# A causal attention with a soft mixture of experts on one core: a new hand-written order of its operations, ordered turns between POOL and VectorE, a third query buffer, the combine softmax in the expert stage, and output in full rows

## The chip, the core and the metric

The kernel runs on one core of a Trainium2 chip. A core has a matrix engine (TensorE; PE in the profile, its weight loads PEld), three elementwise engines (VectorE or DVE, ScalarE or ACT, GpSimd or POOL), and SyncE (SP), which here only issues transfers to the 16 DMA engines. Each engine works through its own instructions in order; between engines there are semaphores. SBUF is the memory of 128 partitions that the engines work on, PSUM is what TensorE writes, in banks of 2 KB a partition. The metric is device time in microseconds of one execution.

## The reference

```python
# q, k, v: (8, 8, 576, 64) = B, H, S, D;  all float32
scores = 1/sqrt(D) * q @ k.T          # causal mask, softmax over keys
local = softmax(scores) @ v
q_p = where(q > 0, q, exp(q) - 1) + 1
mem_out = (q_p @ M_prev) / (q_p . z_prev + 1e-6)
g = sigmoid(beta)                      # one a head
attn = g * mem_out + (1 - g) * local   # -> x: (4608, 512), heads beside each other
# soft mixture of experts: 8 experts, 4 slots each
logits = x @ phi                       # (4608, 32)
d = softmax(logits, axis=0); slot_input = d.T @ x
slot_out[e] = relu(slot_input[e] @ w1[e]) @ w2[e]      # w1 (512, 1024), w2 (1024, 512)
c = softmax(logits, axis=1)            # the combine softmax
out = c @ slot_out                     # (4608, 512)
```

## The kernel before

**Attention.** The 64 heads are worked through as 32 pairs (`n` = 0 to 31: 8 batches of 4 pairs; a pair fills 128 partitions with two heads of 64). For each pair three loads come in on SyncE: q, k (`qk`) and v (`vv`, with M_prev beside it). POOL splits q and k each into a rounded part and a remainder (`op_qhi`, `op_kn` by line 363, `op_qlo` line 394, `op_kl` line 400; into the one tile `X` and the one tile `K2`), so that the scores are three matmuls (line 409, in two groups sA and sB, each in the two banks-of-two `psS0` and `psS1`). VectorE adds the mask and takes the extreme of each row (`op_max`, line 444), out of PSUM; ScalarE takes the exponentials with their sums (`op_exp`, line 453). TensorE transposes the result (`op_t`, line 545), and ScalarE or VectorE copies it out of PSUM (`op_te`, lines 358 and 361) into the one tile `at`, from which the products with v are made (`op_av`, line 572).

**The two normalizers and FR.** Neither part is divided before its product. From the sums (`op_rec`) and the memory norm, factors of a row each are made, turned to lie along a row (`op_rt`, `op_rf`), written to DRAM (`op_rrw`, three transfers, lines 472 and 473), and read back to all partitions (`op_rrr`, line 477: two transfers of 288 KB, tile `FR`, one buffer). FR has two uses: it scales the finished product (`op_mo` line 602, `op_xe` line 607), and its other half multiplies the features (`op_qn`, line 526, one instruction a head, on VectorE or POOL), into the part `C` of `at`, which takes the memory product into the same matmul `av.A`.

**The features.** `op_qmin` (line 482 on ScalarE, 484 on VectorE) writes min(q, 0) into one of two `qp` buffers (`n % 2`), `op_qexp` (line 487, ScalarE) takes its exp, `op_qphi` (line 491, VectorE) adds max(q, 0). Both inputs of `op_qphi` and of `op_qn` lie in SBUF. From the features `op_norm` (line 497, TensorE) makes the memory norm; `op_neps` scales it out of PSUM, `op_nmk` (line 508, POOL or VectorE) masks it, `op_nred` (lines 512 and 513) reduces it, `op_nrw` and `op_nrg` (517, 521, 522) take it through DRAM into `nG`, which `op_rf` uses.

**The slots.** Whenever a quarter of rows (512 of the 4608; `c0` to `c7`) is finished, `op_x1` makes its logits, `op_x1l` to `op_x1d` a running softmax over rows, `op_x3` and `op_x4` add to the slot inputs. `op_x2m`, `op_x2e`, `op_x2s` (lines 656 to 673: two VectorE instructions, one exp, four VectorE instructions), `op_x5` (a transpose, line 702) and `op_x5e` (a copy) make the combine softmax of that quarter, ready and turned, in `cT`. This is done so for seven quarters; the logits of the last two stay in `lt2`. `op_y1` to `op_y12` do the last half quarter and close the sums.

**The order.** All of this is one list, `SEQ` (lines 34 to 285): an entry names an operation, its pair or quarter behind the @, and the PSUM bank behind the colon. The program is emitted in the order of the list, and `pin()` (line 849) fixes it: on each engine every instruction is kept behind the one emitted ahead of it. `EV` says which engine (a, v, p for ScalarE, VectorE, POOL) does an operation that more than one can do. SyncE's transfers, weights (`w.`) too, stand in the same list. A pair takes about 78 entries.

**The experts.** 64 weight tiles of 512 KB (rows of 4 KB) are needed. 28 go to buffers of their own during attention, 17 to the attention's buffers as these come free, 19 to the first of the 28 once the first layer has used them. The first layer (`f1`, line 893), transposes (`f1t`, line 901) and the second layer (`f2`, line 910) follow each other on TensorE; the second layer is done for each half of the 512 output columns in turn (`dh` = 0, 1). In between stand `c1` (lines 914 to 927) and `c2`, which do the combine softmax of the quarters 7 and 8 with one transpose each way. `g1`, `g2` spread a finished half to `so`, and `comb(dh, t4)` (line 943) makes 512 rows of it: eight matmuls (line 949), one copy on ScalarE and one on VectorE, and one transfer of 512 KB in rows of 256 numbers, 1 KB (line 951).

## Time and profile before

| | |
|---|---|
| runs before | 533.03, 526.08, 535.86 us; median 533.03 us |
| the profiled execution | 531.52 us, of which the span from the first to the last instruction 529.4 us |
| mean granted TensorE clock | 0.964 |
| busy: PE, PEld, DVE, ACT, POOL | 452.6, 281.7, 405.2, 342.6, 195.1 us |
| moved | 86.2 MB read from HBM, 9.88 MB written |
| costliest groups | ScalarE exp (L453) 166.6 us, VectorE max (L444) 136.4, products with v (L572) 119.5, transposes (L545) 116.8, scores (L409) 93.1 |
| POOL | L400 47.4 us, L526 46.3, L394 45.4, L363 21.5 and 25.0 |

How to read the rows. A group has its line, engine, operation, the tiles out<-in, shapes, xcount, then busy time and the mean of one in ns, then the idle time of the engine just before it and what ended that. A row of waits has the waiting engine, tile and line, what it waited for, then us in total, times, and the longest. A row of windows has start:end, length, and for each engine busy us and (xinstructions), then the granted clock, the mean busy share of the DMA engines, and GB/s. A row of the timeline has its start, its duration, engine, line, operation, tiles, and in brackets the idle time before it with what ended it. A row by tile has durations ns as min/median/max, then the first and last start in us. "The chain" is the work that ended last, followed back from the end.

### The profile page before, as it was taken

The page shows a single profiled execution, that of the slowest core. Times are in us where ns is not written, and L with a number is a line of the kernel's source. Part 1 is how long each engine was busy: PE and PEld are TensorE (multiplying, and loading weights), DVE is VectorE, ACT ScalarE, POOL GpSimd, SP SyncE. Part 2 cuts the span into 40 slices and gives each one's busy share as a digit, 9 for nine tenths or more (in the row PEclk, how much of TensorE's full clock was granted, in tenths as well). Part 3 has the DMA queues.
Part 4 walks back from the last instruction along what each step waited for, and adds up shares of the span by engine and source line. Part 5 has one row for each costly group of instructions (what it writes and reads, how often), then busy time and mean ns, then how long its engine had stood idle before and what let it go on. Part 6 is the DMA issues. An engine that isn't in the chain of part 4 may idle for free.

```text
span 529.4 us, 13465 instructions
## 1 busy us (share of the span) xinstructions
PE 452.6 (85%) x4874; PEld 281.7 (53%) x4874; DVE 405.2 (77%) x1253; ACT 342.6 (65%) x983; POOL 195.1 (37%) x191
## 2 busy tenths in 40 slices
...
GB/s 218 109 114 163 126 151 251 97 113 180 106 83 164 145 233 169 92 247 112 162 153 250 89 189 117 187 114 145 141 164 167 125 156 241 357 361 407 337 293 303
DMA packets 44192, 96.96 MB, mean 183 GB/s; under 512 B 9184, under 2 KB 19424, under 8 KB 44128
## 3 DMA queue, kind: packets, MB, share of 16 engines
...
q10 hardware_dynamic: 288, 0.09, 0.1%
HBM read 86.22 MB, written 9.88 MB: 182 GB/s over the span
## 4 chain that ended last, share of the span: by engine, by line
PE 34%; DVE 21%; DMA 17%; ACT 9%; issue 7%; POOL 7%; SPq 3%; DVEq 0%; POOLq 0%; ACTq 0%
DMA FR<-rd 11%; PE psS L409 8%; PE psT L545 7%; DVE qp L491 6%; DVE sm L444 5%; PE oa L572 5%; POOL at L526 4%; PE pf L910 3%; ACT qp L482 2%; DVE at L361 2%; PE psT L497 2%; ACT qp L487 2%; PE pf L893 2%; PE pp L949 2%; ACT at L358 2%
## 5 line engine op out<-in xcount | busy, mean ns | idle before, releaser
L453 ACT ACTIVATE sm<-sm,nm 128x192 f32<-128x192 f32 (+4 forms) x288 | 166.6, 581 | 12.3 <-DVE nm L444 11.2
L444 DVE CUSTOM_DVE_ANT_0 sm<-psS,rm 128x320 f32<-128x320 f32 (+4 forms) x288 | 136.4, 509 | 13.2 <-PE psS L409 10.1
L572 PE MATMUL oa<-at,vv 128*32 128x512 f32 (+3 forms) x1280 | 119.5, 474 | 4.4 <-DVE at L526 2.3
L545 PE MATMUL psT<-cs,sm 128*128 128x128 f32 x768 | 116.8, 290 | 7.1 <-ACT at L358 2.4
L358 ACT COPY at<-psT 64x256 f32<-64x256 f32 (+3 forms) x223 | 91.0, 418 | 34.3 <-PE psT L545 16.7
L545 PEld LDWEIGHTS psT<-cs,sm 128*128 128x128 f32 x768 | 87.6, 147 | 40.4 <-issue 13.3
L526 POOL TENSOR_TENSOR at<-qp,FR 64x576 f32<-64x576 f32 x32 | 46.3, 1446 | 153.5 <-DMA FR<-rd 122.7
L409 PE MATMUL psS<-K,X 64*128 64x256 f32 (+2 forms) x960 | 93.1, 330 | 9.5 <-DVE nm L444 7.4
L409 PEld LDWEIGHTS psS<-K,X 64*128 64x128 f32 x960 | 75.2, 193 | 27.8 <-issue 17.2
L361 DVE COPY at<-psT 64x256 f32<-64x256 f32 (+3 forms) x169 | 74.5, 455 | 11.6 <-PE psT L545 5.5
L572 PEld LDWEIGHTS oa<-at,vv 128*32 128x32 f32 x1280 | 35.3, 110 | 42.8 <-issue 25.8
L453 ACT ACTIVATION_READ_ACCUMULATOR sm<-sm,nm 128x1 f32 x288 | 54.8, 190 | 0.0
L491 DVE SCALAR_TENSOR_TENSOR qp<-qk,qp 128x576 f32<-128x576 f32 x32 | 42.2, 1320 | 10.2 <-ACT qp L487 4.6
L400 POOL TENSOR_TENSOR K<-qk,K 128x576 fp32r<-128x576 f32 x32 | 47.4, 1482 | 1.2
L394 POOL TENSOR_TENSOR X<-qk,X 128x512 fp32r<-128x512 f32 x32 | 45.4, 1418 | 0.8
L482 ACT ACTIVATE qp<-qk 128x576 f32<-128x576 f32 x27 | 18.5, 684 | 39.8 <-POOL at L526 24.1
L363 POOL TENSOR_SCALAR X<-qk 128x512 fp32r<-128x512 f32 x32 | 21.5, 673 | 60.4 <-PE psS L409 34.4
L526 DVE TENSOR_TENSOR at<-qp,FR 64x576 f32<-64x576 f32 x32 | 37.9, 1183 | 3.2 <-DMA FR<-rd 2.9
L497 PE MATMUL psT<-qp,qk 128*32 128x144 f32 x256 | 15.2, 310 | 24.9 <-DVE qp L491 18.8
L363 POOL TENSOR_SCALAR K<-qk 128x576 fp32r<-128x576 f32 x32 | 25.0, 782 | 8.7 <-DMA qk<-in_k_dram 4.6
L502 ACT ACTIVATE rn<-psT,rm 128x144 f32<-128x144 f32 x19 | 9.0, 471 | 29.7 <-PE psT L497 28.2
L487 ACT ACTIVATE qp<-qp 128x576 f32<-128x576 f32 x32 | 21.9, 684 | 9.3 <-DVE qp L484 8.5
...
## 6 DMA issues: line engine op xcount, KB each, us to landing
...
```

Of the source, the lines that this page charges most:

```text
L358: nc.scalar.copy(o, i)
L361: nc.vector.tensor_copy(out=o, in_=i)
L363: ENG = dict(a=act, v=dve, p=lambda o, i: nc.gpsimd.tensor_scalar(out=o, in0=i, scalar1=1.0, scalar2=1.0, op0=ALU.mult, op1=ALU.mult))
L394: nc.gpsimd.tensor_tensor(out=X[:, 1, :], in0=st[n]["q"][:, 64:576], in1=X[:, 0, :].bitcast(F32), op=ALU.subtract)
L400: nc.gpsimd.tensor_tensor(out=K2[:, 1, :], in0=kt[:, 0:S], in1=K2[:, 0, :].bitcast(F32), op=ALU.subtract)
L409: nc.tensor.matmul(ps[h][:, a:e], X[ROW[h], x, 128 * i - 128:128 * i], K2[ROW[h], y, k0:k0 + e - a], start=(x, y) == (0, 0), stop=(x, y) = ...
L444: nc.vector.tensor_tensor_reduce(out=smt(n, i, h), in0=src, in1=msk, op0=ALU.add, op1=ALU.min, scale=-0.125, scalar=3.0e38, accum_out=s["n ...
L453: nc.scalar.activation(sm, sm, AF.Exp, scale=-1.0, bias=s["nm"][:, J:J + 1], accum_out=s["sum"][:, J:J + 1])
L491: nc.vector.scalar_tensor_tensor(out=t, in0=st[n]["q"], scalar=0.0, in1=t, op0=ALU.max, op1=ALU.add)
L526: ALU_ENG[ev(f"qn.{h}", n)].tensor_tensor(out=C[r, h, :], in0=st[n]["qp"][r], in1=FR[r, 1, :], op=ALU.mult)
L545: nc.tensor.transpose(out=ps[:, 128 * x:128 * x + 128], in_=win(n, i, h, c), identity=ident)
L572: nc.tensor.matmul(o[r, c0:c1], vt[:, n % 2, c, r], rhs[h], start=start, stop=stop)
```

## The change

1. **The list** `SEQ` and the engine choice `EV` are new throughout. Two and a half thousand entries stay, but for those of point 4. One stretch, from the scores of pair 12 to those of pair 13, before:

```
sA@12 te.A3y@10 te.A3@10 exp.2h0@11 mo@9 exp.a@11 sa@12 te.A1@10 te.AAy@10 rrr@10 t.A2@10:2 exp.2h1@11 x3.1@c2:0
max.1h0@12 te.A2@10 max.4h1@12 t.B3@10:1 exp.1h1@11 nrg@11 x5@c1:2 max.4h0@12 av.1@10 exp.4h1@11 loadk@13 max.a@12
max.1h1@12 te.B3y@10 x1d@c1 x3e.1@c2 sB@12 rec@11 exp.1h0@12 te.B3x@10 te.B3@10 exp.4h1@12 t.A1@11:0 x5e@c1 max.2h0@12
rt@11:1 exp.4h0@12 av.2@10 max.3h1@12 qn.0@10 rf@11 av.3@10 te.A1@11 max.2h1@12 rrw@11 t.A2@11:2 qn.1@10 x3.0@c2:1
kn@13 max.3h0@12 qmin@12 w.r12@0 ava@10:0 av.4@10 te.A2@11 kl@13 av.A@10 qexp@12 xe@10 qphi@12 t.B1@11:2 x3e.0@c2
mo@10 qhi@13 norm@12:0 te.B1@11 t.B3@11:1 qlo@13 neps@12 rrr@11 nmk@12 t.B2@11:0 exp.a@12 nred@12 t.A3@11:2 te.B3y@11
exp.2h0@12 te.B3@11
```

and after:

```
sA@12 x4a.1@c1 exp.2h1@11 te.A2@10 te.A3x@10 exp.3h0@11 te.A3y@10 sa@12 max.4h1@12 exp.3h1@11 t.AA@10:1 loadk@13
norm@12:2 max.a@12 av.2@10 te.AAx@10 rec@11 neps@12 max.1h1@12 te.AAy@10 exp.a@12 nmk@12 rt@11:0 max.1h0@12 t.B1@11:2
rf@11 exp.1h0@12 max.4h0@12 t.A1@11:1 rrw@11 te.B1@11 x3.1@c2:0 nred@12 exp.1h1@12 sB@12 qn.0@10 te.A1@11 nrw@12
qn.1@10 w.r9@0 av.3@10 kn@13 max.3h1@12 loadq@14 qmin@13 ava@10:2 av.A@10 max.3h0@12 qhi@13 x3e.1@c2 xe@10 t.B3@11:1
qexp@13 kl@13 mo@10 t.AA@11:0 te.B3@11 t.A3@11:2 te.B3y@11 exp.3h1@12 rrr@11 te.B3x@11 av.1@11 te.AAy@11 qlo@13
exp.3h0@12 te.A3@11 te.AAx@11 max.2h1@12 t.A2@11:1 te.A3y@11 nrg@12 exp.4h0@12 max.2h0@12 t.B2@11:0 te.A2@11
```

2. **Turns.** For qhi, qlo, kn, kl, qphi, qn and nmk, wherever two that follow each other in the list are on different ones of POOL and VectorE, the later waits for the earlier by a semaphore (`turn`). The list after has 123 such changes of engine. All qmin go to ScalarE (27 of 32 before), qphi can be on either engine and stays on VectorE in all 32; of the 64 qn 34 are on POOL (32 before); of the copies `te` 180 are on VectorE (165 before).

3. **Third query buffer**: `qp` has three buffers, `n % 3`.

4. **Combine softmax behind the experts.** `op_x2m`, `op_x2e`, `op_x2s`, `op_x5`, `op_x5e` and the second transpose of `op_x2` are gone. The logits stay in `cT`, and `c1`/`c2` do all nine quarters in the expert stage in batches of 4, 4 and 1.

5. **Output in full rows.** The weight buffers are allocated as pairs (`wv`). For the rows of `t4` < 2 (`EARLY`) both halves go out as before; for the seven others the two halves of the columns are put into one tile, and one transfer of 1 MB in rows of 2 KB goes out after the second half.

6. **Smaller.** The factors are laid out in 24 rows, so that `op_rrw` is two transfers in place of three; the DRAM tiles `nd` are three fixed ones whose ones are written at the start by three small transfers on ScalarE's queue.

```diff
-    qps = big.tile([128, 2, S], F32, name="qp")
+    qps = big.tile([128, 3, S], F32, name="qp")
...
+    nds = [drm.tile([2, 1088], F32, name=f"nd{i}", bufs=1) for i in range(3)]
...
+        for nd in nds:
+            nc.scalar.dma_start(out=nd[:, S:1088].rearrange("h (r x) -> h r x", x=128), in_=nG[0][0:8])
         nc.vector.memset(den, 0.0)
+        for t in sums:
+            nc.vector.memset(t, 1.0)
...
     def op_rrw(n):
         rf = st[n]["rf"]
-        rd = st[n]["rd"] = drm.tile([2, 2, S], F32, name="rd")
-        for t in range(2):
-            nc.sync.dma_start(out=rd[:, t, 64:S].rearrange("h (i x) -> h i x", i=4), in_=rf[9 * t:9 * t + 8])
-        nc.sync.dma_start(out=rd[:, :, 0:64].rearrange("h t x -> t h x"), in_=rf[8:18:9].rearrange("t (h x) -> t h x", h=2))
+        rd = st[n]["rd"] = drm.tile([2, 2 * S], F32, name="rd")
+        nc.sync.dma_start(out=rd[:, 64:1088].rearrange("h (r x) -> h r x", x=128), in_=rf[0:16])
+        nc.sync.dma_start(out=rd.rearrange("h (t x) -> t h x", x=64)[0:18:17], in_=rf[16:21:4].rearrange("t (h x) -> t h x", h=2))
...
     def op_qmin(n):
-        st[n]["qp"] = qps[:, n % 2]
+        st[n]["qp"] = qps[:, n % 3]
...
     def op_x2(qd):
...
-        if qd < 7:
-            nc.tensor.transpose(out=ps[:, 128:256], in_=d["lt"], identity=ident)
...
+    def wv(x):
+        if x // 2 == len(wdb):
+            wdb.append(wres.tile([128, 2048], F32, name=f"w{x // 2}"))
+        return wdb[x // 2][:, 1024 * (x % 2):1024 * (x % 2) + 1024]
...
+    port = [None]
+
+    def turn(i0, e):
+        for i in list(nc.cur_bb.bb.instructions)[i0:]:
+            if i.engine not in (mybir.EngineType.DVE, mybir.EngineType.Pool):
+                continue
+            if port[0] and port[0][0] != e:
+                tc.add_manual_dep(i, port[0][1], mybir.DependencyInfo(mybir.DependencyClass.Sync, mybir.DependencyReason.DATA), reason="port")
+            port[0] = (e, i.name)
+
...
         a = [int(x) if x.isdigit() and f not in ("w", "max", "exp") else x for x in a]
+        i0, pe = len(nc.cur_bb.bb.instructions), f in ("qhi", "qlo", "kn", "kl", "qphi", "qn", "nmk") and n != "y"
         if n == "y":
             ops[f](*(a or [0]))
         else:
             ops[f](int(n.lstrip("c")), *a)
+        if pe:
+            turn(i0, "p" if f[0] == "k" or f in ("qhi", "qlo") else ev(name.split("@")[0], int(n)))
     si = y["si"]
...
-    stage = [len(order) - nw + x % (NRES - len(order) + nw) for x in range(2 * NQ)]
+    nl = len(order) - nw
+    homes = [wdb[i // 2] for i in range(nl + nl % 2, NRES - 1, 2)] + [pieces[x][:, 0:2048] for x in PARTS if x in pieces]
+    single = [pieces[x] for x in ("X", "K2", "vv", "xk")]
...
-    def c1(qd):
+    cq_ = [(0, 4, at[:, 2048:2560]), (4, 8, acc), (8, 9, at[:, 2048:2560])]
+
+    def c1(x):
+        a, b, t = cq_[x]
+        w = 128 * (b - a)
+        c = cc[x] = t[:, 0:w]
         ps = psP.tile([128, 2, 512], F32, name="pp")[:, 0]
-        nc.tensor.transpose(out=ps[:, 0:128], in_=lt2[:, qd - 7, :], identity=ident)
-        lk = ps[:, 0:128].rearrange("a (j s) -> a j s", s=32)
-        m4 = sml.tile([128, 4], F32, name="m4")
-        nc.vector.reduce_max(out=m4, in_=lk, axis=AX.X)
-        c = cc[qd] = sml.tile([128, 4, 32], F32, name=f"c{qd}", bufs=1)
-        nc.vector.tensor_tensor(out=c, in0=lk, in1=m4.rearrange("a (j x) -> a j x", x=1).broadcast_to([128, 4, 32]), op=ALU.subtract)
+        for i in range(a, b):
+            nc.tensor.transpose(out=ps[:, 128 * (i - a):128 * (i - a) + 128], in_=cT[:, i, :], identity=ident)
+        g = lambda z: z.rearrange("a (j s) -> a j s", s=32)
+        one_ = lambda z: z.rearrange("a (j x) -> a j x", x=1).broadcast_to([128, 4 * (b - a), 32])
+        m4 = sml.tile([128, 16], F32, name="m4")[:, 0:4 * (b - a)]
+        nc.vector.reduce_max(out=m4, in_=g(ps[:, 0:w]), axis=AX.X)
+        nc.vector.tensor_tensor(out=g(c), in0=g(ps[:, 0:w]), in1=one_(m4), op=ALU.subtract)
         nc.scalar.activation(c, c, AF.Exp)
-        s4 = sml.tile([128, 4], F32, name="s4")
-        nc.vector.reduce_sum(out=s4, in_=c, axis=AX.X)
+        s4 = sml.tile([128, 16], F32, name="s4")[:, 0:4 * (b - a)]
+        nc.vector.reduce_sum(out=s4, in_=g(c), axis=AX.X)
         nc.vector.tensor_scalar(out=s4, in0=s4, scalar1=1e-9, scalar2=None, op0=ALU.add)
         nc.vector.reciprocal(out=s4, in_=s4)
-        nc.vector.tensor_tensor(out=c, in0=c, in1=s4.rearrange("a (j x) -> a j x", x=1).broadcast_to([128, 4, 32]), op=ALU.mult)
-
-    def c2(qd):
+        nc.vector.tensor_tensor(out=g(c), in0=g(c), in1=one_(s4), op=ALU.mult)
+
+    def c2(x):
+        a, b, t = cq_[x]
         ps = psP.tile([128, 2, 512], F32, name="pp")[:, 0]
-        nc.tensor.transpose(out=ps[:, 0:128], in_=cc[qd].rearrange("a j s -> a (j s)"), identity=ident)
-        act(cT[:, qd, :], ps[:, 0:128])
-
+        for i in range(a, b):
+            nc.tensor.transpose(out=ps[:, 128 * (i - a):128 * (i - a) + 128], in_=cc[x][:, 128 * (i - a):128 * (i - a) + 128], identity=ident)
+        act(cT[:, a:b, :].rearrange("a q x -> a (q x)"), ps[:, 0:128 * (b - a)])
 
     def g1(dh):
         nc.vector.tensor_scalar(out=ogs[:, dh], in0=po[dh][:, 0:256], scalar1=dt, scalar2=None, op0=ALU.mult)
...
     def comb(dh, t4):
-        o = wres.tile([128, 4, 256], F32, name=f"w{stage[NQ * dh + t4]}")
+        if t4 < EARLY:
+            o = single[2 * t4 + dh].rearrange("a (u d) -> a u d", u=4)
+        else:
+            full = homes[t4 - EARLY].rearrange("a (u d) -> a u d", u=4)
+            o = full[:, :, 256 * dh:256 * dh + 256]
         for half in range(2):
             ps = psP.tile([128, 2, 512], F32, name="pp")
             for v2 in range(2):
                 r = slice(64 * half + 32 * v2, 64 * half + 32 * v2 + 32)
                 nc.tensor.matmul(ps[:, v2, 0:256], cT[r, t4, :], so[r, dh], start=True, stop=True)
             (act, dve)[half](o[:, 2 * half:2 * half + 2, :], ps[:, :, 0:256])
-        nc.sync.dma_start(out=out[512 * t4:512 * t4 + 512, 256 * dh:256 * dh + 256].rearrange("(u a) d -> a u d", a=128), in_=o)
+        d = out[512 * t4:512 * t4 + 512, :].rearrange("(u a) d -> a u d", a=128)
+        if t4 < EARLY:
+            nc.sync.dma_start(out=d[:, :, 256 * dh:256 * dh + 256], in_=o)
+        elif dh:
+            nc.sync.dma_start(out=d, in_=full)
 
     f1(0, 0)
     f1(0, 1)
     f1t(0, 0)
-    c1(7)
-    c1(8)
+    c1(0)
     f1(1, 0)
     f1t(0, 1)
-    c2(7)
-    c2(8)
+    c1(1)
     f1(1, 1)
+    c2(0)
     f1t(1, 0)
     f2(0, 0, 0)
     f1t(1, 1)
     for x in range(len(order) - nw):
-        wload(nw + x, wres.tile([128, 1024], F32, name=f"w{x}"))
+        wload(nw + x, wv(x))
+    c2(1)
+    c1(2)
     f2(0, 0, 1)
     f2(0, 1, 0)
+    c2(2)
     f2(0, 1, 1)
     g1(0)
     f2(1, 0, 0, (0,))
```

More of the change, by code (lines that the diff above doesn't have):

```diff
@@ new lines @@
+max.1h0@16 nmk@16 sB@16 rf@15 x3e.1@c3 nred@16 qn.0@14 rrw@15 te.B1@15 exp.4h1@16 t.A2@15:0 max.2h1@16 t.A1@15:2
+nrw@16 kn@17 max.3h0@16 exp.2h1@16 ava@14:1 te.A1@15 av.4@14 te.A2@15 qhi@17 av.A@14 xe@14 qmin@17 max.3h1@16 kl@17
+w.r16@0 t.B3@15:2 mo@14 exp.3h0@16 t.A3@15:0 qexp@17 max.2h0@16 t.B2@15:1 qlo@17 rrr@15 te.A3y@15 av.1@15 qphi@17
+te.B3@15 exp.3h1@16 sA@17 te.A3@15 nrg@16 te.A3x@15 te.B2@15 te.B3y@15 exp.2h0@16 te.B3x@15 sa@17 max.4h1@17
+exp.1h0@16 t.AA@15:0 loadv@16 t.B1@16:1 te.AAx@15 loadk@18 exp.1h1@16 max.a@17 max.4h0@17 norm@17:2 te.B1@16 av.3@15
```

562 lines of the change are left out of this document (268 added, 294 removed).

## The prediction

> **What bounds the kernel now.** I read the page first (busy shares, chain), then the windows by stage, then the waits of each engine inside the attention stage, and last the rows of the lines that the change touches. All sums are made against the profiled execution: 531.52 us, of which 529.4 us is the span. The median of the three runs is 533.03 us, 1.51 us more, so 1.5 us is added at the end.
>
> ```profile
> span 529.4 us, 13465 instructions
> ...
> PE 452.6 (85%) x4874; PEld 281.7 (53%) x4874; DVE 405.2 (77%) x1253; ACT 342.6 (65%) x983; POOL 195.1 (37%) x191
> ...
> PE 34%; DVE 21%; DMA 17%; ACT 9%; issue 7%; POOL 7%; SPq 3%; DVEq 0%; POOLq 0%; ACTq 0%
> DMA FR<-rd 11%; PE psS L409 8%; PE psT L545 7%; DVE qp L491 6%; DVE sm L444 5%; PE oa L572 5%; POOL at L526 4%; PE pf L910 3%; ACT qp L482 2%; DVE at L361 2%; PE psT L497 2%; ACT qp L487 2%; PE pf L893 2%; PE pp L949 2%; ACT at L358 2%
> ```
>
> The chain is not one engine's. One loop stands out: the transfer of FR (11%), the POOL product that uses it (at L526, 4%), the ScalarE relu and exp (qp L482 and L487, 2% each), the VectorE step (qp L491, 6%) and the norm matmul (L497, 2%): 27% of 529.4 us, some 143 us.
>
> ```profile
> core 0: us, PE busy (x) PEld busy (x) DVE busy (x) ACT busy (x) POOL busy (x), PEclk, DMA share, GB/s
> 0.00:14.00 14.00, 8.13 (x36) 3.81 (x37) 8.57 (x24) 4.38 (x12) 5.80 (x11) 0.98 0.61 208
> 14.00:440.00 426.00, 374.77 (x4040) 241.34 (x4041) 363.29 (x1149) 313.59 (x912) 186.88 (x178) 0.97 0.52 151
> 440.00:468.50 28.50, 21.88 (x253) 13.54 (x251) 14.62 (x42) 10.12 (x34) 2.46 (x2) 0.94 0.91 325
> 468.50:510.00 41.50, 39.64 (x479) 18.32 (x478) 12.51 (x29) 9.00 (x18) 0.00 (x0) 1.00 0.95 358
> 510.00:529.40 19.40, 8.21 (x74) 4.64 (x74) 6.27 (x10) 5.55 (x10) 0.00 (x0) 0.81 0.85 283
> ```
>
> The windows split the span. In attention (14 to 440) TensorE is busy 374.8 of 426 us, 88%, and idle 51.2; VectorE is busy 363.3. In the experts (468.5 to 510) TensorE is busy 39.6 of 41.5. In the last stretch it is done early and the DMA engines work on.
>
> ```profile
> engine line waited for: us in total, times, longest us
> PE psT L497 <- DVE qp L491: 18.8, 19, 1.5
> PE psS L409 <- DVE nm L444: 7.4, 7, 3.4
> PE psT L497 <- DVE xt L607: 4.1, 4, 1.4
> PE psT L572 <- DVE at L526: 3.7, 4, 1.2
> ```
> ```profile
> ACT qp L482 <- POOL at L526: 24.1, 13, 3.8
> ```
> ```profile
> POOL at L526 <- DMA FR<-rd: 109.6, 21, 9.9
> ```
>
> These are the waits of TensorE, ScalarE and POOL from 14 to 440 us. Of TensorE's 51.2 us idle, 18.8 are the norm matmul waiting for qphi. ScalarE waits 24.1 us to overwrite a qp buffer that POOL still needs, and POOL holds it because it waits 109.6 us for FR. So a late FR reaches TensorE through the two-deep query buffer.
>
> **Third query buffer and the looser list: -15.** With `n % 3`, qmin of a pair waits for the products qn of three pairs back, not two. In the list, counted over pairs 4 to 28, qn stands 7.5 entries ahead of the qmin that overwrites its buffer in the old list and 13 to 15 in the new one; from qmin to the norm matmul there are 14 entries before and 40 after; from rrr (issue of FR) to qn 37 and 42; from nrw to rf 49 and 74.
>
> ```profile
> L418 PE MATMUL psS<-qk x64: 222/275/473, 10.1 to 426.4; 128*128 128x64 f32 x64
> ```
>
> This matmul comes twice a pair, so a pair takes (426.4 - 10.1) / 31 = 13.4 us, for about 78 entries, and 26 more entries between qmin and norm are about 4.5 us of cover against waits of at most 1.5 us (TensorE) and 3.8 us (ScalarE). The 18.8 us row is the ceiling and 0 the floor, if the stall only moves to the next use of FR, the matmul on C. I take four fifths, 15, as the cover exceeds the longest wait. What is late next is FR itself for av.A and mo, which no extra buffer loosens.
>
> **Waits between POOL and DVE: -3, between +25 and -14.**
>
> ```profile
> L491 DVE SCALAR_TENSOR_TENSOR qp<-qk,qp x32: 757/1218/1986, 5.3 to 430.9; 128x576 f32<-128x576 f32 x32
> L526 POOL TENSOR_TENSOR at<-qp,FR x32: 1394/1419/1867, 31.8 to 442.1; 64x576 f32<-64x576 f32 x32
> L526 DVE TENSOR_TENSOR at<-qp,FR x32: 734/808/4079, 33.6 to 453.7; 64x576 f32<-64x576 f32 x32
> ```
> ```profile
> L491 DVE SCALAR_TENSOR_TENSOR qp<-qk,qp 128x576 f32<-128x576 f32 x32 | 42.2, 1320 | 10.2 <-ACT qp L487 4.6 <-POOL X L363 3.6 <-issue 1.5
> L526 DVE TENSOR_TENSOR at<-qp,FR 64x576 f32<-64x576 f32 x32 | 37.9, 1183 | 3.2 <-DMA FR<-rd 2.9
> ```
>
> VectorE's two products with both inputs in SBUF take 757 and 734 ns at best but 1320 and 1183 in the mean, while POOL's spread is 1394 to 1867: VectorE is held while POOL runs. The excess is 32 x 0.563 + 32 x 0.449 = 32.4 us of VectorE. The Trainium skill (SBUF — State Buffer, "Who interferes with whom") says that such an instruction and a GpSimd one that reads SBUF exclude each other, and whoever comes second blocks entirely; the trace agrees (757 against 1320 ns), and by that rule a wait only renames the block, so this part alone would be worth 0.
>
> The change makes these turns explicit: 123 handovers in the list instead of 135 alternations that nothing enforced. A handover itself is cheap where the trace has one:
>
> ```profile
> 168.23 0.43 POOL L508 TENSOR_TENSOR rn<-rn,rm 128x144 f32<-128x144 f32 x1
> ```
> ```profile
> 168.70 0.42 DVE L512 TENSOR_REDUCE rq<-rn 128x9 f32<-128x144 f32 x1
> ```
>
> POOL ends at 168.66 and VectorE starts at 168.70. So the price lies in what stands behind: when qphi or qn waits on VectorE, the max rows (L444) and the copies out of PSUM behind it wait too, and TensorE's banks with them; and now they wait also while POOL itself waits (for FR, or for the scores to free X and K2), where before they were held only while POOL ran. Gain bound: of the 32.4 us the qphi part (18.0) mostly lies on the chain and is already in the -15, so at most the qn part, 14.4, is new. Loss bound: 0.8 us a pair, about one half of a POOL product of 1.42, is 25. The list puts qphi behind POOL's four splits of the same pair, whose results the next scores need as well, so most of the time nothing extra is lost: -3.
>
> **Combine softmax out of attention: -5.**
>
> ```profile
> 477.11 0.29 DVE L921 TENSOR_TENSOR c<-pp,m 128x128 f32<-128x128 f32 x1
> 477.78 0.29 DVE L924 TENSOR_REDUCE s<-c 128x4 f32<-128x128 f32 x1 [0.38 <-ACT c L922]
> 478.10 0.17 DVE L925 TENSOR_SCALAR s<-s 128x4 f32<-128x4 f32 x1
> 478.31 0.18 DVE L926 RECIPROCAL s<-s 128x4 f32<-128x4 f32 x1
> 478.52 0.29 DVE L927 TENSOR_TENSOR c<-c,s 128x128 f32<-128x128 f32 x1
> 478.73 0.28 DVE L919 TENSOR_REDUCE m<-pp 128x4 f32<-128x128 f32 x1
> ```
>
> The same six instructions of one quarter, seen here in the expert stage, are 1.50 us of VectorE; seven quarters leave attention: 10.5 us, with seven copies, seven small exp and 14 transposes at 0.165 each (four in 0.66 us, below), 2.3 us of TensorE. TensorE sets the pace, so its 2.3 count in full; VectorE is on the chain for 21% of the span and busy for 77%, so 10.5 x 0.27 = 2.8. Bounds 2.3 and 12.8.
>
> **The rest of the order: -3.** Of TensorE's idle time 51.2 - 18.8 = 32 us are left, in short waits of many kinds. A new order can shorten or lengthen them, by a third, say, 10 us either way; I take -3. SyncE issues one transfer of 0.6 us less for each pair (rrw 3 to 2), on a queue that is not the bound: 0.
>
> Check: these four give 26, attention 400 us, TensorE 372.5 of 400 = 93%. The whole stage now has 88%.
>
> **Start: +0.5.**
>
> ```profile
> 0.73 0.40 ACTq L343 DMA_DIRECT2D rm<-in_beta_dram  x1
> ```
>
> Three small transfers join ScalarE's queue ahead of the first pair, 0.4 us to issue each, partly while it waits for loads: 0 to +1.2. The two memsets are as small as those there.
>
> **Experts: +2.5.**
>
> ```profile
> 475.50 0.66 PE L901 MATMUL pp<-cs,qp 128*128 128x128 f32 x4
> ```
>
> Here TensorE is the path. Now four transposes belong to c1 and c2; then eighteen, fourteen more: 2.3 us by 0.165 each, and up to 3.5 with pauses. VectorE's and ScalarE's parts of the softmax lie under the matmuls (VectorE is busy 12.5 of 41.5 us; in wider rows the nine quarters cost it less than 9 x 1.5). Were that cover gone, it would cost up to 9 x 1.5 = 13.5 us.
>
> **Output in full rows: +8.**
>
> ```profile
> 480.00:485.00 5.00, 4.75 (x41) 1.78 (x42) 1.24 (x4) 1.24 (x4) 0.00 (x0) 1.00 1.03 419
> 505.00:510.00 5.00, 4.47 (x74) 2.33 (x72) 1.82 (x4) 1.02 (x2) 0.00 (x0) 1.00 1.01 336
> 515.00:520.00 5.00, 4.48 (x47) 2.51 (x40) 3.00 (x6) 3.03 (x6) 0.00 (x0) 1.00 1.00 338
> ```
> ```profile
> 497.35 26.27 SPq L951 DMA_DIRECT2D out_dram<-w  x18
> ```
> ```profile
> 512.40 0.69 DVE L361 COPY w<-pp 128x512 f32<-128x512 f32 x1 [2.08 <-DMA out_dram<-w]
> ```
>
> Weights, in rows of 4 KB, move at 419 GB/s at a share of 1.03, so 407; output, in rows of 1 KB, at 336 to 338 at a share of about 1. Today the first half of the output (nine transfers of 0.524 MB, 4.72 MB) goes out from 497.4 on, beside the second half's matmuls, and the second 4.72 MB from 513.1 (512.40 + 0.69, the second half's first tile): 14.0 us at 338, and the span ends 2.3 us after that. The change sends two transfers early and holds the rest until both halves stand in one tile: 9.44 - 1.05 = 8.39 MB after 513.1. Rows of 2 KB are not in the trace. A 1 KB row takes 48.5 ns on one of 16 engines and a 4 KB row 161; on the line between, a 2 KB row takes 86, or 381 GB/s: 22.0 us, 8.0 more. Bounds: 407 GB/s, 20.6, +6.6; 338 GB/s, 24.8, +10.8. The Trainium skill (DMA: Bandwidth & Descriptors, Specifications) puts line rate at rows of 512 B and up; by that, full rows gain nothing and the term is +10.8. The trace's 338 against 407 does not agree with it.
>
> **Sum.** -15 - 3 - 5 - 3 + 0.5 + 2.5 + 8 = -15. 531.5 - 15 = 516.5, and 1.5 to the median: **518 us**, 2.8% under 533.03.
>
> **The rivals.**
>
> *The stall only moves* (FR late at av.A): buffer -4, handovers 0, softmax -5, rest 0, and +11 behind: +2, **535 us**. For it: FR is 11% of the chain, and its path (rf, DRAM, broadcast) is hardly shorter. Against it: TensorE's waits for the qn products are only 3.7 in the row above (L572), against 18.8 behind qphi.
>
> *VectorE stands behind POOL* (the other side): its in-order queue, held at qphi and qn by semaphores, keeps the max rows and the copies back. 0.8 us a pair is +25.6, the buffer's gain halves to -8, softmax -5, behind +11: +24, **557 us**. It decides slower from 10.7 = 11 - 13 + 32x, 0.4 us a pair. For it: POOL waits 109.6 us for FR in the row above, and now VectorE's qn may follow it. Against it: VectorE is held 32.4 us already.
>
> *Attention reaches the pace of TensorE*: 372.5 us of work at 97% is 384, -42, behind +11: -31, **502 us**. For it: the busiest engine has 51 us idle in short waits. Against it: VectorE is nearly as full (363).
>
> *The list does not do what it says*: the handovers are real waits in the code, and the buffer is there; I give it no share of its own.
>
> **How the numbers follow.** Forecast 0.53 (509 to 528 on its own), moved stall 0.17, VectorE behind POOL 0.12, TensorE's pace 0.18. About 2% (10.7 us) is what a measurement of this kernel can tell from no change: its three runs spread from 526.08 to 535.86. Under 522.4 lie 0.18 and seven tenths of the forecast: faster 0.55; within 2% the rest of it and the moved stall: 0.33; slower 0.12. The range reaches from just under the fast rival to past the moved stall with its tail at +10.8, 500 to 541, and leaves out mostly the slow rival.
>
> **What the changed profile would show.** Right: the norm matmul's wait for qphi under 5 us, ScalarE's wait for POOL at qmin nearly gone; L491 and the VectorE products near 0.76 us, with VectorE's waits for POOL in their place, under 20 us; attention some 26 us shorter; the second half's first tile some 23 us earlier than 513.1, and 22 us of output behind it instead of 14; 370 to 390 GB/s in the output. Wrong: FR heading TensorE's waits, L444 waiting for banks behind a held qphi, or a tail that is no longer than today's.

## The result, and the profile after

The changed kernel takes 504.63 us (median of four runs, 502.58 to 509.71) against 529.76 us for the kernel before on the same chip (526.08 to 535.86). The ratio is 0.956, with a 95% interval of 0.943 to 0.969. The forecast was 518 us, within 500 to 541. Ratios here and below leave out runs that lie more than 1.5% above the fastest of their kernel, so they can differ from the quotient of the medians.

The page of the changed kernel, its busy times, then the chain by engine. The lines of attention stand 6 higher than before (qphi L491 is now L497, the product qn L526 is L532, the max rows L444 are L450):

```profile
span 500.8 us, 13360 instructions
PE 440.7 (88%) x4874; PEld 280.8 (56%) x4874; DVE 379.6 (76%) x1229; ACT 333.1 (67%) x956; POOL 186.6 (37%) x196
PE 17%; DVE 2%; ACT 1%; issue 1%; DVEq 0%
```

This chain must be read with care: followed back from the last output transfer it covers a fifth of the span and breaks off, so it says nothing about attention. The windows by stage do:

```profile
14.00:400.00 386.00, 353.18 (x3970) 233.88 (x3970) 335.31 (x1125) 301.35 (x886) 181.02 (x185) 0.98 0.61 172
400.00:428.10 28.10, 25.06 (x310) 15.57 (x313) 16.31 (x46) 11.04 (x34) 1.06 (x1) 1.00 0.77 258
428.10:472.40 44.30, 42.85 (x493) 19.85 (x492) 17.20 (x35) 10.75 (x20) 0.00 (x0) 0.96 0.78 303
472.40:500.80 28.40, 11.56 (x74) 7.23 (x74) 6.71 (x10) 5.55 (x10) 0.00 (x0) 0.56 0.81 295
```

Attention up to the first expert matmul now ends at 428.1 us where it ended at 468.5: 40.4 us less. The experts take 44.3 us instead of 41.3 (468.5 to 509.8), and from the last product of the second half to the end it is 28.4 us instead of 19.6. TensorE's busy time over attention (14 to the first expert matmul) fell from 374.8 + 21.9 = 396.7 to 353.2 + 25.1 = 378.2 us, although only about 2 us of its work was taken away (the estimate of the prediction).

The waits of TensorE, ScalarE, POOL and VectorE from 14 to 400 us, one fence each:

```profile
PE psS L415 <- DVE nm L450: 4.8, 9, 1.0
...
PE psT L503 <- DVE qp L497: 0.5, 1, 0.5
```
```profile
ACT sm L458 <- DVE nm L450: 22.1, 25, 3.7
ACT qp L488 <- DVE at L532: 12.3, 12, 2.6
```
```profile
POOL rn L514 <- DVE rn L510: 53.8, 12, 9.7
...
POOL at L532 <- DMA FR<-rd: 15.6, 8, 4.5
```
```profile
DVE at L532 <- POOL at L532: 14.3, 12, 3.0
```

The norm matmul's wait for qphi (18.8 us before, from 14 to 440 us) is down to 0.5. POOL's wait for FR (109.6) is down to 15.6. In their place stand VectorE's wait for POOL at qn (14.3), ScalarE's wait for VectorE's half of qn before it may overwrite a query buffer (12.3), and a longer wait of ScalarE for the row extremes (22.1, before 8.8). By shape, VectorE's two products out of SBUF, which took 1320 and 1183 ns in the mean, are now near their best:

```profile
L497 DVE SCALAR_TENSOR_TENSOR qp<-qk,qp 128x576 f32<-128x576 f32 x32 | 24.1, 752 | 12.0 <-ACT qp L493 7.3 <-POOL X L400 2.1 <-issue 1.6
L532 DVE TENSOR_TENSOR at<-qp,FR 64x576 f32<-64x576 f32 x30 | 22.3, 743 | 17.5 <-POOL at L532 14.3 <-DMA FR<-rd 2.8
```

At the end, in steps of 5 us:

```profile
465.00:470.00 5.00, 4.44 (x62) 2.64 (x62) 2.67 (x4) 2.25 (x4) 0.00 (x0) 1.00 0.02 3
470.00:475.00 5.00, 3.93 (x58) 2.15 (x50) 0.58 (x2) 0.53 (x2) 0.00 (x0) 1.00 0.00 0
475.00:480.00 5.00, 4.75 (x34) 3.14 (x32) 2.67 (x4) 2.67 (x5) 0.00 (x0) 0.57 0.68 224
480.00:485.00 5.00, 5.00 (x34) 3.09 (x30) 2.68 (x4) 2.04 (x5) 0.00 (x0) 0.50 1.03 373
485.00:490.00 5.00, 0.21 (x2) 0.00 (x0) 0.78 (x2) 0.31 (x1) 0.00 (x0) 0.50 1.03 378
490.00:495.00 5.00, 0.00 (x0) 0.00 (x0) 0.00 (x0) 0.00 (x0) 0.00 (x0) 0.50 1.03 381
```

For ten microseconds (465 to 475) the DMA engines carry next to nothing, where the kernel before was writing its first half at 336 GB/s; then everything goes out at 373 to 381 GB/s.

### The profile page after: what moved, and what is told of

The parts are those of the page before. It is cut to its first block, busy times and chain, and to the rows that moved or that the text cites. A ratio compares the mean times of both kernels' runs of the same rounds, so it can differ in the third digit from the quotient of the medians.

```text
span 500.8 us, 13360 instructions
## 1 busy us (share of the span) xinstructions
PE 440.7 (88%) x4874; PEld 280.8 (56%) x4874; DVE 379.6 (76%) x1229; ACT 333.1 (67%) x956; POOL 186.6 (37%) x196
## 5 line engine op out<-in xcount | busy, mean ns | idle before, releaser
L458 ACT ACTIVATE sm<-sm,nm 128x576 f32<-128x576 f32 (+4 forms) x288 | 166.3, 580 | 23.0 <-DVE nm L450 22.1
L450 DVE CUSTOM_DVE_ANT_0 sm<-psS,rm 128x192 f32<-128x192 f32 (+4 forms) x288 | 137.3, 509 | 11.8 <-PE psS L424 6.1
L578 PE MATMUL oa<-at,vv 128*32 128x512 f32 (+3 forms) x1280 | 114.9, 469 | 0.2 <-ACT at L364 0.2
L551 PE MATMUL psT<-cs,sm 128*128 128x128 f32 x768 | 109.4, 284 | 5.8 <-DVE rf L473 2.7
L364 ACT COPY at<-psT 128x512 f32<-128x512 f32 (+3 forms) x208 | 84.7, 419 | 42.9 <-PE psT L551 22.2
L367 DVE COPY at<-psT 128x256 f32<-128x256 f32 (+3 forms) x184 | 82.3, 458 | 8.6 <-ACT at L364 4.6
L532 POOL TENSOR_TENSOR at<-qp,FR 64x576 f32<-64x576 f32 x34 | 48.1, 1416 | 36.0 <-DMA FR<-rd 15.6
L578 PEld LDWEIGHTS oa<-at,vv 128*32 128x32 f32 x1280 | 35.5, 109 | 31.5 <-issue 19.3
L514 POOL TENSOR_TENSOR rn<-rn,rm 128x144 f32<-128x144 f32 x27 | 11.7, 435 | 109.4 <-DVE rn L510 53.8
L532 DVE TENSOR_TENSOR at<-qp,FR 64x576 f32<-64x576 f32 x30 | 22.3, 743 | 17.5 <-POOL at L532 14.3
L497 DVE SCALAR_TENSOR_TENSOR qp<-qk,qp 128x576 f32<-128x576 f32 x32 | 24.1, 752 | 12.0 <-ACT qp L493 7.3
L488 ACT ACTIVATE qp<-qk 128x576 f32<-128x576 f32 x32 | 21.9, 683 | 14.9 <-DVE at L532 12.3
L608 DVE TENSOR_TENSOR xt<-oa,FR 128x448 f32<-128x448 f32 (+7 forms) x60 | 23.8, 434 | 3.3 <-PE oa L578 3.2
L450 DVE DVE_READ_ACCUMULATOR2_ANT nm<- 128x1 f32 x288 | 23.3, 81 | 0.0
```

Of the source, the lines that this page charges most:

```text
L364: nc.scalar.copy(o, i)
L367: nc.vector.tensor_copy(out=o, in_=i)
L450: nc.vector.tensor_tensor_reduce(out=smt(n, i, h), in0=src, in1=msk, op0=ALU.add, op1=ALU.min, scale=-0.125, scalar=3.0e38, accum_out=s["n ...
L458: nc.scalar.activation(sm, sm, AF.Exp, scale=-1.0, bias=s["nm"][:, J:J + 1], accum_out=s["sum"][:, J:J + 1])
L497: ALU_ENG[ev("qphi", n)].scalar_tensor_tensor(out=t, in0=st[n]["q"], scalar=0.0, in1=t, op0=ALU.max, op1=ALU.add)
L532: ALU_ENG[ev(f"qn.{h}", n)].tensor_tensor(out=C[r, h, :], in0=st[n]["qp"][r], in1=FR[r, 0:S], op=ALU.mult)
```

## The experiments

The result lies between the forecast and the fast rival, so the sum had to be taken apart. The theory of the prediction: the buffer frees the path, the turns only rename a block. Against it: the turns cost much, and something else pays for that. All runs are on one core, each beside the kernel before on its own chip. "Old list" is SEQ and EV of before, less the entries of the combine softmax that no longer exist, in the otherwise changed kernel.

| kernel | median us | ratio [95%] | first expert matmul at | last product | span |
|---|---|---|---|---|---|
| before | 529.76 | 1 | 468.5 | 509.8 | 529.4 |
| before, three query buffers | 520.55 | 0.979 (medians) | 453.2 | 496.2 | 516.3 |
| old list, no turns, two buffers | 537.46 | 1.013 [0.996, 1.030] | 458.9 | 501.6 | 529.8 |
| old list, no turns | 526.10 | 0.984 [0.979, 0.990] | 450.0 | 492.7 | 521.0 |
| old list, no turns, early FR | 527.07 | 1.008 [1.000, 1.015] (medians 0.992) | 452.0 | 494.7 | 523.3 |
| old list | 538.79 | 1.012 [1.008, 1.017] | 464.0 | 506.7 | 535.0 |
| changed | 504.63 | 0.956 [0.943, 0.969] | 428.1 | 472.4 | 500.8 |
| changed, halves at once | 496.62 | 0.931 [0.925, 0.936] | 431.2 | 476.8 | 496.4 |
| changed, no turns | 488.77 | 0.917 [0.914, 0.919] | 413.4 | 458.7 | 486.9 |
| changed, no turns, halves at once | 477.61 | 0.905 [0.895, 0.916] | 413.4 | 456.1 | 475.6 |

The last three columns come from one profiled execution each, while the runs of one kernel can lie 2% apart (before: 526 to 536 us). A difference of a few us between two rows is therefore not exact.

**No turns.** The waits between POOL and VectorE are left out; list, buffers and all else stay.

```diff
-        if pe:
-            turn(i0, "p" if f[0] == "k" or f in ("qhi", "qlo") else ev(name.split("@")[0], int(n)))
```

> The changed kernel without the semaphores between POOL and VectorE, nothing else changed. If a wait only renames a block (the prediction's view): within 1% of the changed kernel, 500 to 510 us, with qphi on VectorE back from a mean of 752 ns to some 1200. If the turns are themselves a large part of the gain (rival): 512 to 525 us.

488.77 us, under both ranges: neither had the turns as a loss. They cost 15.9 us by the medians, 13.9 by the spans. VectorE's products without turns, by shape:

```profile
L532 DVE TENSOR_TENSOR at<-qp,FR 64x576 f32<-64x576 f32 x30 | 26.7, 891 | 3.3 <-DMA FR<-rd 3.0
L497 DVE SCALAR_TENSOR_TENSOR qp<-qk,qp 128x576 f32<-128x576 f32 x32 | 25.3, 792 | 8.3 <-ACT qp L493 7.0 <-issue 0.9 <-POOL K L406 0.3
```

What the turns save is 32 x 0.040 + 30 x 0.148 = 5.7 us of VectorE, because the new list already keeps most of these instructions apart. In exchange they make VectorE stand 14.3 us for POOL at qn and others behind it.

**Halves at once.** Each half row goes out as soon as it stands, as before the change, in rows of 1 KB.

```diff
-            full = homes[t4 - EARLY].rearrange("a (u d) -> a u d", u=4)
-            o = full[:, :, 256 * dh:256 * dh + 256]
+            o = homes[t4 - EARLY][:, 1024 * dh:1024 * dh + 1024].rearrange("a (u d) -> a u d", u=4)
...
-        if t4 < EARLY:
-            nc.sync.dma_start(out=d[:, :, 256 * dh:256 * dh + 256], in_=o)
-        elif dh:
-            nc.sync.dma_start(out=d, in_=full)
+        nc.sync.dma_start(out=d[:, :, 256 * dh:256 * dh + 256], in_=o)
```

> The changed kernel, but both halves of every output row go out on their own as soon as they are ready, in rows of 1 KB. If the tail is set by the bytes that are held back (the prediction's view): the end comes 8 to 9 us earlier, 494 to 498 us, all stages ahead of it as they were. If rows of 1 KB cost as much as holding back (rival): 502 us or more.

496.62 us, as the view of the prediction had it. From the last product to the end it is 496.4 - 476.8 = 19.6 us, as before the change, against 28.4: the full rows cost 8.8 us.

**Old list, with and without turns.** SEQ and EV of before in the changed kernel; the second run also without `turn`.

> The old list and the old choice of engines in the changed kernel (three query buffers, turns, combine softmax behind the experts, full rows). If the buffer itself is what frees the query loop: attention and ramp-down end near 445 us, 515 to 520 us in all. If it needs the new list, because ScalarE's qmin stands right behind qn in the old list (rival): they end at 460 to 475 us, 530 to 545 us in all.

> As the run before (old list in the changed kernel), and without the turns. If turns cost in a list that was not laid out for them: 5 to 15 us under that run. If they are neutral: within 5 us of it.

The first run, 538.79 us, lies in the range of its rival, but not for the rival's reason: what holds it back are the turns, as the second run shows (526.10), and not the buffer (below). Without turns the old list reaches its first expert matmul at 450.0 us, the new one at 413.4: the order of the work, which here means the list with its choice of engines, is worth 36.6 us, by far the largest part. With the old list the turns cost 14.0 us there (464.0), with the new one 14.7 (428.1), so the two do not need each other. In the old list (its lines stand some 230 lower: L295 is qn, L260 qphi) the two products, by shape, and POOL's wait from 14 to 400 us are

```profile
L295 DVE TENSOR_TENSOR at<-qp,FR 64x576 f32<-64x576 f32 x32 | 36.0, 1125 | 3.1 <-DMA FR<-rd 2.9
L260 DVE SCALAR_TENSOR_TENSOR qp<-qk,qp 128x576 f32<-128x576 f32 x32 | 35.8, 1120 | 5.6 <-ACT qp L256 5.5
```
```profile
POOL at L295 <- DMA FR<-rd: 102.3, 22, 8.3
```

The same windows of 362 us show what the order did to TensorE, first with the old list, then with the new:

```profile
14.00:376.00 362.00, 323.70 (x3556) 207.72 (x3560) 310.89 (x998) 277.55 (x808) 174.02 (x165) 0.99 0.56 160
```
```profile
14.00:376.00 362.00, 342.48 (x3885) 227.24 (x3885) 329.29 (x1093) 292.99 (x862) 183.92 (x184) 0.99 0.64 181
```

In the same time 3885 matmuls instead of 3556, idle time of 19.5 us instead of 38.3, and 88.2 ns of busy time for each matmul instead of 91.0 (342.48 / 3885, 323.70 / 3556), at the same granted clock of 0.99: the busy time shrinks together with the waits. A single matmul is not faster (a transpose of the exponentials has a mean of 281 ns with either list), so the matmuls follow each other more closely. Over all of attention, 14 us to the first expert matmul, TensorE's idle time falls from 48.3 to 24.3 us and its busy time from 387.7 to 375.1; these two make the 36.6 us. And most of the idle time that went stood in front of two matmuls, the norm (L266, then L503) and the product on `C` (L341, then L578), first with the old list, then with the new:

```profile
L266 PE MATMUL psT<-qp,qk 128*32 128x144 f32 x256 | 15.3, 307 | 16.6 <-DVE qp L260 9.4 <-issue 3.4 <-DVE xt L376 2.7
L341 PE MATMUL psT<-at,vv 128*32 128x64 f32 x256 | 12.1, 225 | 8.7 <-DVE at L295 5.9 <-DVE at L130 1.8 <-POOL at L295 1.0
```
```profile
L503 PE MATMUL psT<-qp,qk 128*32 128x144 f32 x256 | 14.9, 306 | 3.4 <-issue 3.0 <-DVE qp L497 0.4
L578 PE MATMUL psT<-at,vv 128*32 128x64 f32 x256 | 11.4, 225 | 2.0 <-POOL at L532 1.4 <-DVE rf L473 0.4 <-DVE at L532 0.2
```

That is 13.2 and 6.7 us, on the path of the features that the prediction names; most of it remained after the buffer, and the order took it away.

**The buffer.** Once taken from the changed kernel with the old list and without turns, once added to the kernel before by itself:

```diff
-        st[n]["qp"] = qps[:, n % 3]
+        st[n]["qp"] = qps[:, n % 2]
```
```diff
-    qps = big.tile([128, 2, S], F32, name="qp")
+    qps = big.tile([128, 3, S], F32, name="qp")
...
-        st[n]["qp"] = qps[:, n % 2]
+        st[n]["qp"] = qps[:, n % 3]
```

> The old list, without the waits between POOL and VectorE, with two query buffers in place of three; all else as changed. To be held against the same kernel with three buffers, 526.1 us. The prediction's step (the third buffer itself frees the norm matmul from waiting for qphi): slower by 8 to 15 us, 534 to 541, with the norm matmul's wait for qphi near 19 us and ScalarE's wait at qmin near 24 us again. Rival (the old list was planned for two buffers, so a third is worth little by itself, and what the change gained comes from the order): slower by 0 to 3 us, 525 to 530, and the waits at qmin and the norm matmul differ by under 8 us between the two.

> The kernel before with a third query buffer and nothing else: its own list, in which both halves of qn stand 2 to 11 entries ahead of the qmin two pairs on. The prediction's step (the buffer frees the norm matmul's 18.8 us): 518 to 525 us, ratio 0.97 to 0.985, ScalarE's wait for POOL at qmin nearly gone and the norm's wait for qphi under 10 us. Rival (the old order was planned for two buffers, the buffer by itself is worth little): 530 to 535 us, the norm's wait for qphi over 14 us.

With two buffers in place of three the time goes from 526.1 to 537.5 us and the first expert matmul from 450.0 to 458.9; added to the kernel before, the buffer takes 531.88 us (before on that chip) to 520.55, and the first expert matmul from 468.5 to 453.2. Both times lie where the prediction's step had them, even in an order planned for two buffers. The waits of TensorE and ScalarE with two buffers, 14 to 400 us:

```profile
PE psT L266 <- DVE qp L260: 14.8, 18, 1.8
```
```profile
ACT qp L251 <- POOL at L295: 21.7, 13, 4.1
```

With three, in the same order, and then in the kernel before with three:

```profile
PE psT L266 <- DVE qp L260: 9.4, 13, 1.2
```
```profile
PE psT L497 <- DVE qp L491: 8.0, 11, 1.1
```

ScalarE's wait for POOL at qmin is gone in both. So the buffer takes a third to a half of the norm's wait (14.8 to 9.4, and from 16.9 in the kernel before, in the same window, to 8.0), not four fifths; the rest went with the order (0.5 us in the changed kernel). And the new order can't be had without the buffer: in the old list qn.0 stands 2 to 11 entries ahead of the qmin two pairs on, in the new list 55 to 75 entries behind it, when with two buffers its features would be gone.

**Which turns cost.** Only those in which VectorE waits; only those in which POOL waits; all without qn among the operations; only those in which a qn is the one that waits. The last are 32 of the 123, and 26 of these 32 are VectorE's half of qn waiting for POOL's.

```diff
-            if port[0] and port[0][0] != e:
+            if port[0] and port[0][0] != e and e == "v":
```
```diff
-            if port[0] and port[0][0] != e:
+            if port[0] and port[0][0] != e and e == "p":
```
```diff
-        i0, pe = len(nc.cur_bb.bb.instructions), f in ("qhi", "qlo", "kn", "kl", "qphi", "qn", "nmk") and n != "y"
+        i0, pe = len(nc.cur_bb.bb.instructions), f in ("qhi", "qlo", "kn", "kl", "qphi", "nmk") and n != "y"
```
```diff
-            if port[0] and port[0][0] != e:
+            if qn and port[0] and port[0][0] != e:
...
-            turn(i0, "p" if f[0] == "k" or f in ("qhi", "qlo") else ev(name.split("@")[0], int(n)))
+            turn(i0, "p" if f[0] == "k" or f in ("qhi", "qlo") else ev(name.split("@")[0], int(n)), f == "qn")
```

> The changed kernel with only those waits in which VectorE waits for POOL; POOL no longer waits for VectorE. Against 504.6 with all and 488.8 with none. Theory A (the cost is VectorE's in-order queue, held at qn and qphi with the max rows and the evictions behind it): 498 to 504 us, VectorE's wait for POOL at the product qn near 14 us. Theory B (the cost is POOL's turn: the splits of keys and its own products held until VectorE has had its instruction, so scores and FR come late): 489 to 492 us. If each side has a half: 494 to 498.

> The changed kernel with only those waits in which POOL waits for VectorE; VectorE no longer waits for POOL. Theory A (VectorE's held queue): 489 to 492 us, as with no waits. Theory B (POOL held): 498 to 504 us, POOL's waits for VectorE at rn, X and qn as long as with all waits, near 95 us in sum. If each side has a half: 494 to 498. If the loss needs both (a chain of alternating turns), both this and the other one lie within 3 us of 488.8.

> The changed kernel with the waits between POOL and VectorE at the splits, the products qphi and the masks, but none at the two halves of the product qn. Against about 504.6 us with all and 488.8 with none. Theory A (the loss sits at qn: VectorE's half is held behind POOL's half, which waits for FR; its wait of 14.3 us for POOL is the loss): 488 to 492 us. Theory B (the loss sits at the splits and qphi, where POOL and VectorE wait for the scores and for each other pair by pair): 498 to 504 us. Half and half: 494 to 497.

> The changed kernel with waits between POOL and VectorE only where an instruction of the product qn is one of the neighbours that waits; the splits, qphi and masks run when they are ready. Theory A (the loss sits at qn): 498 to 504 us, VectorE's wait for POOL at qn near 14 us. Theory B (it sits elsewhere): 488 to 492. Half and half: 494 to 497.

VectorE's waits alone: 500.30 us, 0.944 [0.928, 0.959]. POOL's alone: 497.87 us, 0.942 [0.931, 0.952]. By the medians both are dearer than none (488.77), by 11.5 and 9.1 us, and which of the two is dearer the intervals don't say. With the waits of qn alone it is 506.97 us, 0.951 [0.946, 0.956], as much as with all of them. Without qn the four runs are 489.48, 489.94, 497.41 and 497.51 us; the ratio of 0.921 [0.917, 0.924] is that of the lower two, so the other turns by themselves cost between 1 and 9 us, and these runs don't say which. So the 32 waits of qn are enough for the whole loss; that the others are free is not shown, and the losses don't add. One of the 32 in the changed kernel, by the timeline (start, duration, and in brackets the idle time before it):

```profile
199.35 0.37 DVE L367 COPY at<-psT 64x256 f32<-64x256 f32 x1
200.74 1.40 POOL L532 TENSOR_TENSOR at<-qp,FR 64x576 f32<-64x576 f32 x1 [4.47 <-DMA FR<-rd]
202.18 0.75 DVE L532 TENSOR_TENSOR at<-qp,FR 64x576 f32<-64x576 f32 x1 [2.46 <-POOL at L532]
202.85 0.61 DVE L450 CUSTOM_DVE_ANT_0 sm<-psS,rm 128x448 f32<-128x448 f32 x1
202.96 0.69 ACT L488 ACTIVATE qp<-qk 128x576 f32<-128x576 f32 x1 [2.24 <-DVE at L532]
203.07 0.32 PE L578 MATMUL psT<-at,vv 128*32 128x64 f32 x8 [1.97 <-DVE at L532]
```

POOL waits 4.5 us for FR, then takes 1.4 us for its half. VectorE, idle since 199.7, waits for POOL's half to end; ScalarE (2.24 us) and TensorE (1.97) wait for VectorE. The same pair in the run without turns:

```profile
187.72 0.36 DVE L367 COPY at<-psT 64x256 f32<-64x256 f32 x1
188.01 0.74 DVE L532 TENSOR_TENSOR at<-qp,FR 64x576 f32<-64x576 f32 x1
188.35 1.68 POOL L532 TENSOR_TENSOR at<-qp,FR 64x576 f32<-64x576 f32 x1 [3.71 <-DMA FR<-rd]
190.08 0.25 PE L578 MATMUL psT<-at,vv 128*32 128x64 f32 x2 [0.51 <-POOL at L532]
```

The two halves of FR come by two transfers. VectorE's half needs the first and runs before POOL's; the list has POOL's half first, and the turn makes VectorE wait for the second transfer and for POOL. Counted from the copy in the first line, the matmuls on the later half start 2.36 us on without the turn; with it none of those on the two halves starts before 3.72 us, 1.4 us later.

**FR earlier in the old list.** The half of FR that qn uses gets a second buffer, and its transfers stand 8 entries behind the write of the factors instead of behind the product that frees FR.

```diff
+    FQ = [FR[:, 0:S], big.tile([128, S], F32, name="FQ")]
...
+    def op_rrq(n):
+        for h in range(2):
+            nc.sync.dma_start(out=FQ[n % 2][ROW[h]], in_=st[n]["rd"][h:h + 1, 0:S].broadcast_to([64, S]))
...
-            nc.sync.dma_start(out=FR[ROW[h]], in_=st[n]["rd"][h:h + 1].broadcast_to([64, 2 * S]))
+            nc.sync.dma_start(out=FR[ROW[h], S:2 * S], in_=st[n]["rd"][h:h + 1, S:2 * S].broadcast_to([64, S]))
...
-        ALU_ENG[ev(f"qn.{h}", n)].tensor_tensor(out=C[r, h, :], in0=st[n]["qp"][r], in1=FR[r, 0:S], op=ALU.mult)
+        ALU_ENG[ev(f"qn.{h}", n)].tensor_tensor(out=C[r, h, :], in0=st[n]["qp"][r], in1=FQ[n % 2][r], op=ALU.mult)
```

> The changed kernel with the old list and no waits between POOL and VectorE (526.1 us, ratio 0.984), in which the half of FR that the product qn uses has two buffers and is fetched 8 entries behind its write, some 19 entries (about 3 us) earlier than in the old list; two more transfers a pair on SyncE. Theory A (what the new list cured is the late FR, for which POOL waits 102 us in the old list and 24 in the new): POOL's wait falls under 50 us and the time by 10 to 25 us, to 501 to 516, ratio 0.94 to 0.965. Theory B (POOL's idle time in front of qn lies off the path, and the new list gains in many short waits instead): POOL's wait falls as well, but the time by under 5 us, ratio 0.975 to 0.995.

POOL's wait falls from 102.3 us to 36.0, and the time doesn't (527.07 us beside 531.27 for the kernel before on that chip; the span is 2.3 us longer than without the early fetch). POOL's and SyncE's waits from 14 to 400 us:

```profile
POOL K L387 <- DMA qk<-in_k_dram: 25.8, 8, 5.8
POOL X L387 <- DMA qk<-in_q_dram: 21.2, 5, 6.5
POOL at L554 <- DMA FR<-rd: 18.4, 6, 3.9
POOL at L554 <- DMA FQ<-rd: 17.6, 9, 4.1
```
```profile
SPq L501 <- DMA rd<-rf: 33.2, 29, 3.6
```

The early fetch holds SyncE's queue until the factors have landed in DRAM, the loads of q and k behind it come late, and POOL waits 47 us for those in the two rows above, where it waited 16 without the early fetch. So this run does not tell the two theories apart: one late transfer stands in place of another, and an early FR on a queue of its own is not tried.

**No turns, halves at once.** The two edits that helped, together.

> The changed kernel without the waits between POOL and VectorE, and with each half row of the output going out as soon as it stands (rows of 1 KB). If the two terms are independent: 488.8 less what the halves gave (504.6 on another chip or 502.6 profiled, to 496.6: 6 to 8), so 481 to 483 us, and the last stretch behind the expert's last product near 20 us. Rival (with the attention shorter the halves' transfers meet more weights still being loaded, so the gain shrinks): 485 to 488 us.

477.61 us, 0.905 [0.895, 0.916] of the kernel before: the fastest of all, and some 3 us under the range for independent terms. The last stretches of its windows:

```profile
413.40:456.20 42.80, 41.27 (x493) 19.75 (x492) 17.27 (x35) 10.74 (x20) 0.00 (x0) 1.00 1.01 381
456.20:475.60 19.40, 8.21 (x74) 4.61 (x74) 6.34 (x10) 5.54 (x10) 0.00 (x0) 0.86 0.86 286
```

Against the span without turns (486.9) it is 11.3 us: 8.8 in the tail (19.4 against 28.2), and 2.5 in the experts (42.8 against 45.3), where the granted clock was 1.00 in this run and 0.94 in the other. So the terms add, and the rest goes with the clock; why that differed is not shown.

## Why the prediction was right and wrong

The sum in steps, each read at the first expert matmul between two kernels that differ by that step: 468.5, buffer to 453.2, softmax and the small edits to 450.0, order to 413.4, turns to 428.1. The experts and the tail are read between the kernel before and the changed one.

| term | predicted | measured |
|---|---|---|
| third query buffer (the list counted with it) | -15 | -15.3, buffer alone (taken from the old list with the other edits, -8.9) |
| combine softmax out of attention | -5 | -3.2 (from the other side, against before with two buffers, -9.6) |
| rest of the order | -3 | -36.6 |
| turns | -3 | +14.7 |
| experts | +2.5 | +3.0 |
| output in full rows | +8 | +8.8 |

- **Buffer and softmax together, and output: right in size.** Buffer and softmax took 18.5 us where 20 were forecast; how they share them depends on which comes first (15.3 + 3.2 or 8.9 + 9.6). (Of the buffer's 15.3 us the medians show 11.3; the granted clock in attention was 0.99 in that profile and 0.97 in that of before.) The buffer's mechanism was right too, though less of the norm's wait went than was thought, and part of its gain is busy time of TensorE (396.7 to 390.0 us over attention), which the term didn't count. Of the experts' 3.0 us only 1.4 show at an equal granted clock of 1.00 (42.7 us with the old list, 41.3 before); in the changed kernel's profile it was 0.96 there. The output term came from the line between a 1 KB and a 4 KB row, 381 GB/s for 2 KB; measured are 373 to 381. By the Trainium skill (DMA: Bandwidth & Descriptors, Specifications) rows of 512 B and up run at line rate, and the tail would have been 10.8 us longer; the traces, 338 GB/s for 1 KB and 381 for 2 KB, don't agree with it.
- **The step that failed for size is "The rest of the order: -3".** It took a third of TensorE's 32 us of other idle time, 10 us either way, as the bound; the order took 24.0 us of idle time, most of it at the norm, which the prediction had given to the term of the buffer and the looser list, and at the product on `C`, which it took as not to be loosened by a buffer. Behind the bound stood the check that TensorE has 372.5 us of work in attention. That busy time is no constant: with the order it fell by 12.5 us (91.0 to 88.2 ns a matmul in the windows above). The order also took 19.8 us off VectorE's two products (36.0 + 35.8 to 26.7 + 25.3), all without a single turn. The whole of attention then comes to 413.4 us, under the fast rival's 426.5 (468.5 - 42).
- **The step that failed in sign is "Waits between POOL and DVE: -3".** Its own figures had the price. The loss was bounded at 0.8 us a pair, and the rival on the slow side named the mechanism, VectorE's queue held at qn, decisive from 0.4 us a pair. Measured are 14.7 / 32 = 0.46 us a pair. That rival's mechanism happened (VectorE's waits alone cost 11.5 us), though POOL's waits alone, which it didn't name, cost 9.1; its total (557 us) didn't come, since the order paid for the turns twice over. What was wrong in the forecast's own argument is the place: it went over qphi behind POOL's splits, and not over qn, whose two halves wait for two transfers and which the turn puts one behind the other. The waits of qn alone cost as much as all of them.
- **The rule weighed there**, that a wait only renames the block (worked out from the Trainium skill, SBUF — State Buffer, "Who interferes with whom"), would have given 0. The block itself is there: with turns the two products take 743 and 752 ns, without them VectorE's half of qn reaches 1.9 us (at 115.24 us, beside POOL's half from 115.11 to 116.53), which is hardly better than a turn. But a block holds VectorE only while POOL works, and a turn holds it also while POOL waits: in the first timeline above VectorE's idle time from 199.7 us on falls for its first 1.0 us into POOL's wait for the second transfer, which VectorE's half doesn't use. A block isn't always short either: the 4079 ns in the prediction's row are VectorE's half held through POOL's qn and the three splits behind it.
- **Start: +0.5** was short as well. The first matmul of line 424 (418 before) starts at 13.8 us in place of 10.1:

```profile
L424 PE MATMUL psS<-qk x64: 222/275/473, 13.8 to 391.2; 128*128 128x64 f32 x64
```

With the small edits, but without waits of POOL's splits for VectorE, it starts at 11.5 to 12.5 us (seven of the profiles); with these waits at 13.6 to 13.9 (five). So the edits cost 1.4 to 2.4 us at the start, which the softmax step above holds, and the turns 1 to 2 us more.
- **The total came out inside the range by luck:** two terms were missed, by -33.6 and +17.7, and the second hid half of the first.
- **The signs in the profile** named beforehand: norm's wait under 5 us (0.5), products near 0.76 us, VectorE's wait for POOL under 20 us (14.3), 370 to 390 GB/s: as said. Attention shorter by 26 us: it was 40.4. The second half's first tile 23 us earlier than 513.1: it stood 37.5 us earlier, at 475.6.

What stays open: which of the order's many moves brings the 36.6 us, and how much of it is the earlier FR, which the run that fetches it early doesn't settle.
